# Pacing the row gathers of a mixture-of-experts kernel by TensorE's progress

## The chip, the cores and the metric

The kernel runs on one core of one Trainium2 chip. The metric is device time in microseconds (us) of one execution. Six participants matter: TensorE (PE in the profile, with its weight loads as PEld), VectorE (DVE), ScalarE (ACT), GpSimd (POOL), the SyncE queue (SP), and the 16 DMA engines that serve all the queues. Each engine works through its own instructions in order, and the engines wait for one another through semaphores.

## What is computed

An attention-like block (retention) is followed by a mixture of eight experts. The reference, cut to what matters:

```python
scores = scale * q @ k.T                       # 8 batches, 8 heads, 576 positions, 64 wide
x = ((scores * Dmat) @ v)                      # as 4608 tokens x 512
noisy = x @ w_gate + log1p(exp(x @ w_noise)) * noise
top2  = two best of 8 experts per token;  top2_w = softmax over the two
for e in range(8):
    h = maximum(x[mask] @ w1[e], 0)            # 512 -> 1024
    out[mask] += top2_w * (h @ w2[e])          # 1024 -> 512
```

Matmuls run in bf16. The noise and the weights decide which tokens an expert gets, so the rows of an expert are only known once the tokens have been routed.

## The kernel before

The attention part goes through 16 units (four pairs of batches, four pairs of heads). After each pair of batches the tokens of that pair are routed (`route`): the two best experts are found, each token gets a place in its experts' lists, the lists are turned into a table of row numbers `xi0` to `xi3`, and the token rows (512 bf16 values and 8 words of payload with the gate weights and places) are written to a scratch tensor `xd` in HBM. The fourth routing is the last; only then are all lists complete.

An expert has room for 1216 tokens, cut into nine pieces of 128 and one of 64. `tiles()` groups pieces into tiles. Nine early tiles of one or two pieces (experts 0 to 2, as far as their lists are sure to be filled by earlier routings) run while the attention part still goes on. Twenty late tiles of two to four pieces hold the other 65 pieces; they lie behind the last routing. `fetch` brings the rows of a tile's pieces together, one indirect DMA for each piece, issued by POOL (line 964 of the profile) into a place of class `xg`. There are 24 such places; the last routing uses ten of them first. TensorE transposes the rows (L982) and a copy makes the tile's `xT`; for experts 6 and 7 a DMA transpose on the SP queue (L972) does that instead. Then come the first product (`up`, L1036, for early tiles; `wide`, L1062, for late ones), the relu on ACT or DVE (L1045, L1047), and the second product (`second`, L1113), whose steps are woven between the first-product steps of the next tile. `finish` scales the result: rows of a token's first expert go to a second scratch tensor `yd` (L1147 or L1149, then L1153); rows of its second expert are added to what `prev` fetched back from `yd` (an indirect DMA of POOL, L1128, then L1157 on DVE) and are scattered to the output (an indirect DMA of POOL, L1161).

The order of the instructions is not written by hand. `Plan` records operations with a cost each, and `Plan.run` simulates the engines: it picks the operation that can begin first, gives it an engine and a place, and so fixes the order on every engine. What it fixes is the order alone. On the chip an instruction starts when its engine is free and its semaphores allow it, whether that is earlier or later than the simulated time.

Two details matter here. A gather in `fetch` waits for its table, for the written rows of `xd`, and for the last readers of its `xg` place. And `slot()` limits how many `xg` places the gathers may hold in the simulation: 14 while the routing still needs places, and afterwards a number that starts at 5 and grows by one for every two gathers placed:

```python
n = head[b.cls, b.stream]
lim = min(hi, 5 + (n - self.mark.setdefault((b.cls, b.stream), n)) // 2) if b.cls == "xg" else hi
```

Of the kernel before, what the change touches and what calls it, by code (L numbers as in the profile page):

```python
# [15 lines left out]
IOff = bass.IndirectOffsetOnAxis  # L16

P = 128
# [4 lines left out]
DM = 512  # L23
KD = DM // P
KF = F // P
# [4 lines left out]
YOFF = [sum(min(-(-x // P) * P, CAP) for x in FIRST[:e]) for e in range(E + 1)]  # L30
WAIT = (11, 14, 15)
CROSS = 6
CLOSE = ((256, 0, 0, 0, 0, 0, 0, 0), (512, 384, 384, 0, 0, 0, 0, 0), (768, 640, 512, 0, 0, 0, 0, 0))
PLW = 8
XW = DM // 2 + PLW
# [13 lines left out]


class Op:
    __slots__ = ("i", "eng", "fn", "prio", "dma", "port", "preds", "succ", "need", "allocs", "bufs", "fin", "on")


class Plan:
# [5 lines left out]
    BIAS = dict(DVE=1.5, ACT=0.5)  # L61

    def __init__(self):
        self.ops, self.slots, self.fifo, self.quota, self.zone, self.mark = [], {}, {}, {}, {}, {}

    def cls(self, name, tiles, **quota):
        self.slots[name] = [[0.0, None, t, p] for t, p in tiles]
# [6 lines left out]
    def fix(t=None):  # L74
        return Buf(None, None, t)

    def op(self, eng, cost, fn, r=(), w=(), prio=0.0, dma=0, after=(), port=False):
        o = Op()
        o.i, o.fn, o.prio, o.dma, o.port = len(self.ops), fn, prio, dma, port
        o.eng = eng if isinstance(eng, dict) else {eng: cost}  # L80
        o.succ, o.allocs, o.bufs = [], [], []
        preds = set(after)
        for items, wr in ((r, False), (w, True)):
            for it in items:
                b, sub = it if isinstance(it, tuple) else (it, None)
                for s2, o2, w2 in b.acc:
                    if (wr or w2) and (sub is None or s2 is None or s2 == sub):
                        preds.add(o2)
                if b not in o.bufs:
                    o.bufs.append(b)  # L90
        for items, wr in ((r, False), (w, True)):
            for it in items:
                b, sub = it if isinstance(it, tuple) else (it, None)
                if wr:
                    b.acc = [a for a in b.acc if a[1] is o or not (sub is None or a[0] == sub)]
                b.acc.append((sub, o, wr))
        preds.discard(o)
        for b in o.bufs:
            if b.cls is not None:
                if not b.ops:  # L100
                    o.allocs.append(b)
                    self.fifo.setdefault((b.cls, b.stream), []).append(b)
                b.ops.append(o)
                b.left += 1
        o.preds, o.need = preds, len(preds)
        for p in preds:
            p.succ.append(o)
        self.ops.append(o)
        return o

    def run(self):
        free, dma_free, port = {}, {}, [0.0]
        head = {k: 0 for k in self.fifo}
        used = {}
        lanes = {"SP": [], "POOL": []}
# [4 lines left out]
        def slot(b, taken):  # L120
            s = self.slots[b.cls]
            lim = self.quota[b.cls].get(b.stream, len(s))
            lo, hi = self.zone.get((b.cls, b.stream), (0, len(s)))
            if lim < len(s) and all(head[k] >= len(v) for k, v in self.fifo.items()
                                    if k[0] == b.cls and k[1] != b.stream):
                lo, hi = 0, len(s)
                n = head[b.cls, b.stream]
                lim = min(hi, 5 + (n - self.mark.setdefault((b.cls, b.stream), n)) // 2) if b.cls == "xg" else hi
            if used.get((b.cls, b.stream), 0) + sum(t[1].n for t in taken if t[1].cls == b.cls) + b.n > lim:
                return None  # L130
            ok = lambda x: x[1] is None and all(x is not y for t in taken for y in t[0])
            best = None
            for i, x in enumerate(s[:hi]):
                if i < lo:
                    continue
                if b.n == 2:
                    if i % 2 or not (ok(x) and ok(s[i + 1])):
                        continue
                    c, k = [x, s[i + 1]], (max(x[0], s[i + 1][0]), 0)
                elif not ok(x):  # L140
                    continue
                else:
                    c, k = [x], (x[0] + (0.3 if len(s) == 8 and ok(s[i ^ 1]) else 0.0), 1)
                if best is None or k < best[0]:
                    best = k, c
            return best and best[1]

        while ready:
            pick = None
            for o in ready:  # L150
                taken = []
                ok = all(b.cls is None or b.t is not None or b in o.allocs for b in o.bufs)
                if not ok:
                    continue
                for n, b in enumerate(o.allocs):
                    k = (b.cls, b.stream)
                    q = self.fifo[k]
                    m = len([t for t in taken if (t[1].cls, t[1].stream) == k])
                    if q[head[k] + m] is not b:
                        ok = False  # L160
                        break
                    x = slot(b, taken)
                    if x is None:
                        ok = False
                        break
                    taken.append((x, b))
                if not ok:
                    continue
                t0 = max([y[0] for x, b in taken for y in x], default=0.0)
                best = None  # L170
                for e, c in o.eng.items():
                    t = max(t0, free.get(e, 0.0))
                    if o.port and e in ("DVE", "POOL"):
                        t = max(t, port[0])
                    if o.dma and len(lanes[e]) >= 8:
                        t = max(t, lanes[e][-8])
                    for p in o.preds:
                        t = max(t, p.fin + (0.0 if p.on == e and not p.dma else self.LAT))
                    x = t + c + (self.BIAS.get(e, 0.0) if len(o.eng) > 1 else 0.0)
                    if best is None or x < best[0]:  # L180
                        best = x, e, t, c
                _, e, t, c = best
                key = (round(t * 20), o.prio, o.i)
                if pick is None or key < pick[0]:
                    pick = (key, o, e, t, c, taken)
            if pick is None:
                raise RuntimeError("no operation can go on: " + str([(o.i, o.prio) for o in ready[:20]]))
            _, o, e, t, c, taken = pick
            ready.remove(o)
            o.on = e  # L190
            free[e] = t + c
            if o.port and e in ("DVE", "POOL"):
                port[0] = t + c
            o.fin = t + c
            if o.dma:
                x = max(dma_free.get(e, 0.0), t + c)
# [37 lines left out]
class Kernel:  # L234
# [719 lines left out]
    def fetch(self, i, t, prio):  # L954

        pl, nc = self.pl, self.nc
        e, js, early = t
        ident = self.fixed["ident"]
        xi = self.fixed[f"xi{early}"]
        xg = [pl.buf("xg", "exp") for _ in js]  # L960
        rows = 1 + 1152 * (early + 1)
        for x, j in zip(xg, js):
            h, n = HPE * e + j, self.size(j)
            pl.op("POOL", 1.3, lambda _, x=x, h=h, n=n: nc.gpsimd.indirect_dma_start(  # L964
                out=x.t[:n, :], out_offset=None, in_=self.xd[:rows, :], in_offset=IOff(ap=xi.t[:n, h:h + 1], axis=0),
                bounds_check=rows - 1, oob_is_err=False), r=[xi] + self.xd_done[early], w=[x], prio=prio, dma=0.4)
        xT = pl.buf("half" if early < 3 else "big", "xt")
        w, m, off = sum(self.size(j) for j in js), len(js) * P, self.off(js)
        xv = lambda m=m: xT.t.bitcast(BF16)[:, :KD * m].rearrange("p (k s) -> p k s", k=KD)
# [5 lines left out]
        for c in range(0, 0 if e >= CROSS and early == 3 else len(js), 2):  # L975
            p = self.psum("xt")
# [72 lines left out]
    def wide(self, i, t, prio, g2=None):  # L1049
# [5 lines left out]
        for f in range(KF):  # L1055
            p = self.psum("exp")

            def pe(_, f=f, p=p):
                it = g2(f) if g2 else iter(())
                for di in range(KD):  # L1060
                    o = di * F + f * P
                    nc.tensor.matmul(p.t[:, :n], lhsT=w.t[:, o:o + P], rhs=xv()[:, di, :n],  # L1062
                                     start=(di == 0), stop=(di == KD - 1))
                    next(it, None)
                for _ in it:
                    pass
# [40 lines left out]
    def second(self, e, po, hT, c, f):  # L1107


        k = KF // len(hT)  # L1110
        hv = hT[f // k].t.bitcast(BF16).rearrange("p (f s) -> p f s", f=k)[:, f % k]
        o = KD * F + f * DM
        self.nc.tensor.matmul(po.t, lhsT=hv[:, c:c + P], rhs=self.W[e].t[:, o:o + DM],  # L1113
                              start=(f == 0), stop=(f == KF - 1))

    def prev(self, i, t, prio):
        pl, nc = self.pl, self.nc
# [53 lines left out]
    def record(self):  # L1171
# [32 lines left out]
        for i, t in enumerate(ts):  # L1204
            starts.setdefault(t[0], i)
        last = {t[0]: i for i, t in enumerate(ts)}
        ne = len([t for t in ts if t[2] < 3])
        landed = lambda u: [o for o in pl.ops if o.dma and o.prio == u]
        for e, u in enumerate(WAIT):
            self.weights(e, 40 + e, True, landed(u))  # L1210
# [200 lines left out]
```

## Time and profile before

| what | value |
| --- | --- |
| median of 3 runs | 490.4 us (485.36, 490.4, 490.55) |
| the profiled execution | 485.52 us, span from first to last instruction 484.0 us |
| PE busy | 398.0 us, 82% of the span |
| POOL busy | 292.9 us, 61% |
| ACT busy | 246.4 us, 51% |
| DVE busy | 187.5 us, 39% |
| mean granted TensorE clock | 0.926 of full speed |
| gathers of L964 | 80, of 1045 ns each on POOL |
| DMA | 105.32 MB, 218 GB/s over the span |

The page's busy shares are means over very different stages: attention up to about 180 us, the end of the early tiles up to about 228 us, the late tiles up to about 474 us, and a tail of scatters. "Busy" of POOL for an indirect DMA is the time in which POOL prepares the transfer, not the transfer itself. In the view of instructions in order of time, the bracket at the end of a row tells how long the engine had been idle before that row and what ended the wait: an engine and line, a DMA, "issue" (nothing that the profile shows), or "remote" (a semaphore whose update the profile can't put down to an instruction near it).

### The profile page before, as it was taken

The page shows a single profiled execution, that of the slowest core. Times are in us where ns is not written, and L with a number is a line of the kernel's source. Part 1 is how long each engine was busy: PE and PEld are TensorE (multiplying, and loading weights), DVE is VectorE, ACT ScalarE, POOL GpSimd, SP SyncE. Part 2 cuts the span into 40 slices and gives each one's busy share as a digit, 9 for nine tenths or more (in the row PEclk, how much of TensorE's full clock was granted, in tenths as well). Part 3 has the DMA queues.
Part 4 walks back from the last instruction along what each step waited for, and adds up shares of the span by engine and source line. Part 5 has one row for each costly group of instructions (what it writes and reads, how often), then busy time and mean ns, then how long its engine had stood idle before and what let it go on. Part 6 is the DMA issues. An engine that isn't in the chain of part 4 may idle for free. (4 is left out here: it accounts for less than half of the span.)

```text
span 484.0 us, 10610 instructions
## 1 busy us (share of the span) xinstructions
PE 398.0 (82%) x4032; PEld 245.5 (51%) x4032; DVE 187.5 (39%) x499; ACT 246.4 (51%) x431; POOL 292.9 (61%) x361
## 2 busy tenths in 40 slices
PE   1698768729988898149999888999799979999991
PEld 1576657528766665026565434455354434454450
DVE  2755776855892782001133313215025021031231
ACT  3699758657874743026575354745345233244320
POOL 8985779874497365733007747544656746656524
PEclk9889769878999999569999989999999979999997
DMA  7999999999599595423189977695599996645414
GB/s 192 298 261 286 272 238 303 257 245 328 128 319 269 136 256 166 96 75 118 37 291 349 343 248 220 188 369 166 167 310 298 236 217 182 181 150 161 150 55 144
DMA packets 102488, 105.32 MB, mean 218 GB/s; under 512 B 31870, under 2 KB 80511, under 8 KB 102434
## 3 DMA queue, kind: packets, MB, share of 16 engines
q1 hardware_dynamic: 80082, 58.92, 41.8%
q0 software_dynamic: 15264, 36.89, 30.2%
q10 hardware_dynamic: 7088, 8.80, 5.2%
q8 instruction: 32, 0.52, 0.5%
q14 instruction: 22, 0.18, 0.1%
HBM read 83.20 MB, written 26.63 MB: 227 GB/s over the span
## 5 line engine op out<-in xcount | busy, mean ns | idle before, releaser
L1113 PE MATMUL ps<-W,half 128*128 128x512 bf16 x640 | 214.9, 388 | 24.6 <-ACT half L1045 18.1
L1062 PE MATMUL ps<-big,W 128*128 128x512 bf16 (+4 forms) x640 | 190.5, 331 | 5.8 <-issue 5.2
L1045 ACT ACTIVATE half<-ps 128x512 bf16<-128x512 f32 (+5 forms) x180 | 87.1, 505 | 158.2 <-PE ps L1062 70.2
L964 POOL DMA_INDIRECT xg<-xd,xi x80 | 83.6, 1045 | 57.0 <-issue 20.4
L1113 PEld LDWEIGHTS <-half 128*128 128x128 bf16 x640 | 62.2, 99 | 99.4 <-ACT half L1045 18.9
L1062 PEld LDWEIGHTS <-W 128*128 128x128 bf16 x640 | 63.1, 99 | 55.5 <-issue 9.1
L1157 DVE SCALAR_TENSOR_TENSOR half<-ps,xg,half 128x512 f32<-128x512 f32 (+1 forms) x39 | 29.0, 747 | 73.5 <-PE ps L1113 42.1
L1161 POOL DMA_INDIRECT out_dram<-half,xg x39 | 39.1, 1003 | 29.6 <-issue 16.6
L1128 POOL DMA_INDIRECT half<-yd,xg x39 | 39.8, 1022 | 11.9 <-issue 11.9
L515 DVE TENSOR_TENSOR half<-ps,mask 128x512 bf16<-128x512 f32 x64 | 40.1, 682 | 16.4 <-PE ps L507 14.4
L269 ACT ACTIVATE half<-ps 128x1024 bf16<-128x1024 bf16 (+1 forms) x36 | 35.1, 990 | 15.5 <-PE ps L482 9.3
L457 POOL TENSOR_TENSOR half<-big,tab 128x1024 bf16<-128x1024 f32 x16 | 31.0, 1935 | 14.6 <-PE ps L482 6.2
L464 POOL TENSOR_TENSOR half<-big,tab 128x512 bf16<-128x512 f32 x32 | 33.6, 1066 | 1.5 <-issue 1.5
L542 PE MATMUL ps<-half,half 128*128 128x128 bf16 (+1 forms) x128 | 30.2, 322 | 2.4 <-POOL half L464 2.2
L1157 DVE SCALAR_TENSOR_TENSOR half<-ps,gm,half 128x512 f32<-128x512 f32 x6 | 4.5, 751 | 70.9 <-ACT half L1147 64.4
L1036 PE MATMUL ps<-half,W 128*128 128x256 bf16 (+1 forms) x288 | 29.1, 255 | 2.9 <-ACT half L269 2.5
L482 PE MATMUL ps<-ident__69,half 128*128 128x128 bf16 x256 | 22.3, 247 | 11.0 <-ACT half L449 5.9
L544 PE MATMUL ps<-vz,half 128*128 128x128 bf16 x128 | 25.4, 251 | 6.3 <-ACT vz L269 4.6
L1147 ACT ACTIVATE half<-ps,xg 128x512 f32<-128x512 f32 (+1 forms) x29 | 19.9, 685 | 16.4 <-PE ps L1113 11.0
L1036 PEld LDWEIGHTS <-W 128*128 128x128 bf16 x288 | 24.0, 98 | 7.0 <-issue 3.4
L554 ACT ACTIVATE tb<-ps 64x256 bf16<-64x256 f32 x56 | 21.1, 376 | 11.0 <-PE ps L544 9.8
L482 PEld LDWEIGHTS <-half 128*128 128x128 bf16 x256 | 18.9, 113 | 12.0 <-ACT half L449 5.9
(177 smaller groups left out, 462.8 us busy)
## 6 DMA issues: line engine op xcount, KB each, us to landing
big<-in_moe_w_dram SPq DMA_DIRECT2D x40, 512.0 KB
big<-in_k_dram SPq DMA_DIRECT2D x32, 256.0 KB
big<-in_q_dram SPq DMA_DIRECT2D x16, 512.0 KB
big<-in_v_dram SPq DMA_DIRECT2D x32, 256.0 KB
yd<-half SPq DMA_DIRECT2D x26, 256.0 KB
W<-in_moe_w_dram POOLq DMA_DIRECT2D x12, 512.0 KB
xd<-xg ACTq DMA_DIRECT2D x16, 264.0 KB
yd<-half ACTq DMA_DIRECT2D x15, 256.0 KB
```

What stands on the lines that cost most here:

```text
L269: self.nc.scalar.activation(out, in_, Act.Copy)
L464: self.eng(e).tensor_tensor(o, i, t, Alu.mult)
L482: nc.tensor.transpose(v[:, hp, x, :], i[:, y, hp * P:(hp + 1) * P], ident.t)
L515: nc.vector.tensor_tensor(S.t.bitcast(BF16).rearrange("p (h c x) -> p h c x", h=2, c=2)[:, h], p[h].t.rearrange("p (c x) -> p c x", c=2), ...
L964: pl.op("POOL", 1.3, lambda _, x=x, h=h, n=n: nc.gpsimd.indirect_dma_start(out=x.t[:n, :], out_offset=None, in_=self.xd[:rows, :], in_offs ...
L1036: nc.tensor.matmul(pv()[:, f2, :], lhsT=w.t[:, o:o + P], rhs=xv()[:, di, :n], start=(di == 0), stop=(di == KD - 1))
L1045: self.nc.scalar.activation(o, i, Act.Relu)
L1062: nc.tensor.matmul(p.t[:, :n], lhsT=w.t[:, o:o + P], rhs=xv()[:, di, :n], start=(di == 0), stop=(di == KD - 1))
L1113: self.nc.tensor.matmul(po.t, lhsT=hv[:, c:c + P], rhs=self.W[e].t[:, o:o + DM], start=(f == 0), stop=(f == KF - 1))
L1128: pl.op("POOL", 1.3, lambda _, b=b, iy=iy, n=self.size(j): nc.gpsimd.indirect_dma_start(out=b.t[:n, :], out_offset=None, in_=self.yd[:rows ...
L1157: pl.op("DVE", 0.75, lambda _, o=o, b=b, po=po, g=g, n=n: nc.vector.scalar_tensor_tensor(o.t[:n], po.t[:n], g()[:n], b.t[:n], Alu.mult, Al ...
L1161: ins = nc.gpsimd.indirect_dma_start(out=self.out[:, :], out_offset=IOff(ap=io()[:n], axis=0), in_=o.t[:n, :], in_offset=None, bounds_chec ...
```

## The change

The growing limit on `xg` places is removed: once the last routing has taken its places, gathers may hold all 24. In its place comes a pace for the gathers of late tiles other than the first late one (61 of the 80). In the simulation such a gather begins no sooner than 2.2 us after the last paced one. In the program it also waits for the matmul of L1062 or L1113 that was issued last ahead of it in the simulated order: `wide` and `second` note their newest matmul in `self.mm`, and `fetch` adds a semaphore dependency of the gather on it.

```diff
+PACE = 2.2
...
     def run(self):
-        free, dma_free, port = {}, {}, [0.0]
+        free, dma_free, port, paced = {}, {}, [0.0], 0.0
...
                 lo, hi = 0, len(s)
-                n = head[b.cls, b.stream]
-                lim = min(hi, 5 + (n - self.mark.setdefault((b.cls, b.stream), n)) // 2) if b.cls == "xg" else hi
+                lim = hi
...
                 t0 = max([y[0] for x, b in taken for y in x], default=0.0)
+                if o.pace:
+                    t0 = max(t0, paced + o.pace)
...
             free[e] = t + c
+            if o.pace:
+                paced = t
...
-            pl.op("POOL", 1.3, lambda _, x=x, h=h, n=n: nc.gpsimd.indirect_dma_start(
-                out=x.t[:n, :], out_offset=None, in_=self.xd[:rows, :], in_offset=IOff(ap=xi.t[:n, h:h + 1], axis=0),
-                bounds_check=rows - 1, oob_is_err=False), r=[xi] + self.xd_done[early], w=[x], prio=prio, dma=0.4)
+            pace = PACE if early == 3 and i > self.ne else 0.0
+
+            def get(_, x=x, h=h, n=n, pace=pace):
+                ins = nc.gpsimd.indirect_dma_start(
+                    out=x.t[:n, :], out_offset=None, in_=self.xd[:rows, :], in_offset=IOff(ap=xi.t[:n, h:h + 1], axis=0),
+                    bounds_check=rows - 1, oob_is_err=False)
+                if pace:
+                    self.tc.add_manual_dep(ins.ins, self.mm.ins.name, mybir.DependencyInfo(
+                        mybir.DependencyClass.Sync, mybir.DependencyReason.DATA), reason="gathers go at TensorE's pace")
+            pl.op("POOL", 1.3, get, r=[xi] + self.xd_done[early], w=[x], prio=prio, dma=0.4, pace=pace)
...
-                    nc.tensor.matmul(p.t[:, :n], lhsT=w.t[:, o:o + P], rhs=xv()[:, di, :n],
-                                     start=(di == 0), stop=(di == KD - 1))
+                    self.mm = nc.tensor.matmul(p.t[:, :n], lhsT=w.t[:, o:o + P], rhs=xv()[:, di, :n],
+                                               start=(di == 0), stop=(di == KD - 1))
...
-        self.nc.tensor.matmul(po.t, lhsT=hv[:, c:c + P], rhs=self.W[e].t[:, o:o + DM],
-                              start=(f == 0), stop=(f == KF - 1))
+        self.mm = self.nc.tensor.matmul(po.t, lhsT=hv[:, c:c + P], rhs=self.W[e].t[:, o:o + DM],
+                                        start=(f == 0), stop=(f == KF - 1))
```

`self.ne` is the number of early tiles (9), so the late tile with index 9 keeps its four gathers unpaced. The cost that the simulation puts on a gather (1.3 us of POOL) is unchanged.

More of the change, by code (lines that the diff above doesn't have):

```diff
@@ L51 @@
 class Op:
-    __slots__ = ("i", "eng", "fn", "prio", "dma", "port", "preds", "succ", "need", "allocs", "bufs", "fin", "on")
+    __slots__ = ("i", "eng", "fn", "prio", "dma", "port", "preds", "succ", "need", "allocs", "bufs", "fin", "on", "pace")
 class Plan:
@@ L63, in __init__ @@
     def __init__(self):
-        self.ops, self.slots, self.fifo, self.quota, self.zone, self.mark = [], {}, {}, {}, {}, {}
+        self.ops, self.slots, self.fifo, self.quota, self.zone = [], {}, {}, {}, {}
     def cls(self, name, tiles, **quota):
@@ L75, in fix, with op @@
         return Buf(None, None, t)
-    def op(self, eng, cost, fn, r=(), w=(), prio=0.0, dma=0, after=(), port=False):
+    def op(self, eng, cost, fn, r=(), w=(), prio=0.0, dma=0, after=(), port=False, pace=0.0):
         o = Op()
-        o.i, o.fn, o.prio, o.dma, o.port = len(self.ops), fn, prio, dma, port
+        o.i, o.fn, o.prio, o.dma, o.port, o.pace = len(self.ops), fn, prio, dma, port, pace
         o.eng = eng if isinstance(eng, dict) else {eng: cost}
@@ L1206, in record @@
         last = {t[0]: i for i, t in enumerate(ts)}
-        ne = len([t for t in ts if t[2] < 3])
+        self.ne = ne = len([t for t in ts if t[2] < 3])
         landed = lambda u: [o for o in pl.ops if o.dma and o.prio == u]
```

## Prediction

> **What bounds the kernel now.** I first read the page's chain of work that ended last. It covers nothing here, so it names no bound:
>
> ```profile
> span 484.0 us, 10610 instructions
> POOL 0%; issue 0%; POOLq 0%
> ```
>
> So I went to the busy times by stage. A row holds the window, its length, and then the busy time and count of PE, PEld, DVE, ACT and POOL, the granted clock, the DMA share and GB/s.
>
> ```profile
> 192.00:212.00 20.00, 2.19 (x5) 0.39 (x6) 0.52 (x4) 1.96 (x4) 12.89 (x13) 0.56 0.35 88
> 212.00:228.00 16.00, 16.00 (x126) 10.16 (x126) 1.03 (x6) 8.37 (x15) 3.98 (x4) 0.91 0.32 100
> 228.00:474.00 246.00, 233.81 (x1312) 119.13 (x1309) 64.02 (x111) 107.32 (x197) 132.52 (x128) 0.98 0.71 216
> 474.00:484.00 10.00, 0.00 (x0) 0.00 (x0) 0.75 (x1) 0.00 (x0) 3.89 (x5) 0.68 0.35 124
> ```
>
> From 212 to 474 PE is the bound: it is busy 249.8 of 262 us, and every other engine has half its time free or nearly so. The last 10 us are a tail of scatters in which PE does nothing. The row that stands out is the first. For 20 us PE does 2.19 us of work, ACT and DVE do next to nothing, and only POOL works. In the order of time these are the PE, ACT and POOL rows around it (start, busy time, and in brackets the idle time before and what ended it):
>
> ```profile
> 191.40 0.49 PE L1036 MATMUL ps<-half,W 128*128 128x256 bf16 x3 [0.35 <-issue]
> 194.97 1.04 PE L1113 MATMUL ps<-W,half 128*128 128x512 bf16 x2 [3.08 <-issue]
> 203.43 1.04 PE L1113 MATMUL ps<-W,half 128*128 128x512 bf16 x2 [7.42 <-ACT half L1045]
> 211.88 4.18 PE L1113 MATMUL ps<-W,half 128*128 128x512 bf16 x12 [7.42 <-ACT half L1045]
> 194.31 0.60 ACT L1045 ACTIVATE half<-ps 128x512 bf16<-128x512 f32 x1 [3.72 <-remote]
> 202.78 0.60 ACT L1045 ACTIVATE half<-ps 128x512 bf16<-128x512 f32 x1 [7.86 <-remote]
> 211.23 1.08 ACT L1045 ACTIVATE half<-ps 128x512 bf16<-128x512 f32 x2 [7.86 <-remote]
> 184.26 0.96 POOL L964 DMA_INDIRECT xg<-xd,xi  x1 [5.45 <-DVE half L1047]
> 207.59 1.00 POOL L964 DMA_INDIRECT xg<-xd,xi  x1 [0.31 <-issue]
> L964 POOL DMA_INDIRECT xg<-xd,xi x19 | 18.8, 992 | 10.9 <-DVE half L1047 5.5 <-issue 5.2 <-DMA xg<-xd,xi 0.3
> ```
>
> PE waits for a relu of ACT (L1045). ACT waits for the signal that the first-product matmuls are done, and those had been issued by 191.9 (191.40 + 0.49). The last two relus stand in one row at 211.23: their signals came together, although their matmuls are different ones. So the matmuls were not late; the word of them was. In the same time POOL issues 19 gathers with nothing between them, from 184.26 to 208.59, one every 1.30 us ((207.59 - 184.26) / 18). The relus are freed one by one, 8.46 us apart (six or seven gathers), and the last one 2.6 us after the chain's end.
>
> Does that happen elsewhere? I looked for ACT waits ended by "remote" in the late tiles, and for what POOL did before them; and, as a control, for an isolated gather.
>
> ```profile
> ACT half L1045 <- remote: 38.2, 7, 8.5
> 266.06 1.00 POOL L964 DMA_INDIRECT xg<-xd,xi  x1 [0.30 <-issue]
> 279.07 1.00 POOL L964 DMA_INDIRECT xg<-xd,xi  x1 [0.30 <-remote]
> 278.88 0.44 ACT L1045 ACTIVATE half<-ps 128x320 bf16<-128x320 f32 x1 [8.53 <-remote]
> 279.37 0.30 PE L1062 MATMUL ps<-big,W 128*128 128x320 bf16 x1 [2.10 <-issue]
> 333.92 1.05 POOL L1161 DMA_INDIRECT out_dram<-half,xg  x1 [1.83 <-DVE W L271]
> 345.91 1.00 POOL L964 DMA_INDIRECT xg<-xd,xi  x1 [0.30 <-issue]
> 348.31 0.60 ACT L1045 ACTIVATE half<-ps 128x512 bf16<-128x512 f32 x1 [2.25 <-remote]
> 348.96 0.38 PE L1113 MATMUL ps<-W,half 128*128 128x512 bf16 x1 [2.47 <-ACT half L1045]
> 371.65 1.05 POOL L964 DMA_INDIRECT xg<-xd,xi  x1 [0.30 <-issue]
> 388.70 1.00 POOL L964 DMA_INDIRECT xg<-xd,xi  x1 [0.30 <-issue]
> 391.96 1.09 ACT L1045 ACTIVATE half<-ps 128x512 bf16<-128x512 f32 x2 [5.68 <-remote]
> 217.06 1.00 POOL L964 DMA_INDIRECT xg<-xd,xi  x1 [1.30 <-ACT half L1147]
> 218.72 0.60 ACT L1045 ACTIVATE half<-ps 128x512 bf16<-128x512 f32 x1 [0.28 <-PE ps L1036]
> ```
>
> Three more unbroken chains of POOL's indirect DMAs (266.06 to 280.07, 333.92 to 346.91, 371.65 to 389.70; 10 to 14 transfers each) have such a late relu in them or up to 2.3 us behind. The lone gather at 217.06 has none: the relu behind it waits 0.28 us for PE, by name. The seven waits of the summary make 38.2 us of ACT; PE, which has other work at most of them, loses far less. That is a correlation at four places with a control, not a proof. It is what my forecast rests on: **a long unbroken chain of POOL's indirect DMAs holds back PE's signals to ACT.**
>
> **The change part by part.**
>
> *The chain behind the last routing breaks up.* In the changed program 61 of the 80 gathers wait for a matmul. The paced gathers number 20 to 40 wait for matmuls that lie, on the mean, 2.1 us of PE work apart, and all 61 are let go within some 184 us of PE work, 3.0 us apart. Both are longer than the 1.30 us of the chain. Since the matmul waited for stands in PE's order, a stalled PE now stops the gathers, so a chain can't run on while PE stands. Only the first four gathers after the routing are unpaced, and some three more wait for matmuls that are done by then: about seven run from 184.3 to 192 before POOL halts. So I let the first idle gap of PE (3.08) stay, and take away the two of 7.42: **-14.8 us**. The bounds are 0 (nothing goes) and -17.9 (3.08 goes too).
>
> *The clock.* After the hole PE runs slower than it does a little later:
>
> ```profile
> 219.40 3.62 PE L1113 MATMUL ps<-W,half 128*128 128x512 bf16 x16
> ```
>
> Twelve matmuls took 4.18 us at 211.88 (0.348 each) and sixteen took 3.62 here (0.226 each); the windows show the clock granted at 0.56 in the hole and 0.91 behind it. Twelve times 0.122 is **-1.5 us**, if the clock no longer falls. Bounds 0 to -1.5.
>
> *The late tiles.* From 228 to 474 PE is idle for 12.2 us (246 - 233.81). The two gaps shown at 279.37 and 348.96 make 4.6 of it. The new order still has runs of up to six of `prev` and scatter (L1128, L1161), which are not paced, so I take a third of the 12.2: **-4.0 us**. Bounds 0 to -12.2.
>
> *The gathers wait, and POOL with them.* The waits stand in POOL's queue, so the `prev` and scatter behind a halted gather halt too, and behind these the add on DVE (L1157), the free `xg` places, and the writes of `yd` on SP and ACT as far as they share buffers. In the late window POOL is busy 132.52 of 246, so 113 us are free, 1.85 us for each of the 61 paced gathers. Each gather is let go at least 10 us of matmul work ahead of the transposes that read its rows, and a tile's last gather some 196 matmuls ahead of the tile's first product. The trace has no such wait; the nearest row is a gather that waited for its `xg` place:
>
> ```profile
> 214.76 0.99 POOL L964 DMA_INDIRECT xg<-xd,xi  x1 [6.17 <-ACT half L1147]
> ```
>
> POOL stood for 6.17 us there and PE was fully busy in that window (16.00 of 16.00), so a stand of that size has been absorbed once. I put this part at **0**; its upper bound is the second rival's price.
>
> *Moved steps.* Four gathers of an early tile move ahead of the last routing's steps on POOL:
>
> ```profile
> 173.71 1.11 POOL L964 DMA_INDIRECT xg<-xd,xi  x1 [0.17 <-issue]
> 177.75 1.05 POOL L964 DMA_INDIRECT xg<-xd,xi  x1 [0.30 <-issue]
> 163.07 0.24 POOL L737 TENSOR_TENSOR d<-bm,am 128x9 f32<-128x9 f32 x1 [4.12 <-DVE bm L714]
> ```
>
> Three fit into the 4.12 us that POOL idles at 163.07; one falls between two routing steps and may cost up to 1.3 us, which POOL gets back where they stood before (173.71 to 178.80). Three writes of `yd` move ahead of transposes on SP's queue. No row shows PE waiting for either, so both go at **0**, the gather with a bound of +1.3. PE's signals grow from 634 to 646 and POOL's separate waits from 217 to 227, on queues with idle time: 0.
>
> **Sum**, against the profiled execution's own 485.5 us (span 484.0 and 1.5 around it): 485.5 - 14.8 - 1.5 - 4.0 + 0 = 465.2, so **465 us**. That execution lies 4.9 us below the median of the three runs and equals the fastest of them; I keep to it, since its rows carry the sum.
>
> **The rivals.**
>
> *The gathers are innocent* (or the new waits find their matmuls already done and change nothing). The relus were late for a reason of their own, the gathers merely filled the time, and the hole stays: the time is **485 us**. For it: no row shows how a gather could hold a signal back. Against it: the four chains, and the control. The Trainium skill, SBUF — State Buffer, section "SBUF: two separate sides", speaks for this rival: "Engine ports and AXI ports are disjoint. A DMA cannot be slowed by a compute op, and vice versa." By that rule gathers cost ACT nothing, and the sum would be 485. The trace differs with it as far as the 8.53 us wait at 278.88 falls inside a chain.
>
> *POOL now waits for the late word itself* (slower). If PE's signals are late for whatever reason, the gathers, which need PE's signal now, hear of it late as well, and POOL, which is in order, loses that time 61 times. It decides from 1.85 us per gather, the free time above; beyond that `prev`, scatters and gathers fall behind PE. Releases came 1.4 us (346.91 to 348.31) to 2.6 us (208.59 to 211.23) after a chain's end. At 2.5 us the excess is 61 x 0.65 = 40 us, on top of the 465: **about 504 us**. For it: ACT lost 38.2 us to this kind of wait, seven times, and it waits for PE as POOL now will. Against it: without chains no late word was seen (218.72), and the waits of neighbouring gathers overlap.
>
> *Half of it stays* (a smaller gain). The first seven gathers and the copies of the routing before them already make a chain long enough for one more period of 8.46 us: 465 + 8.5, **about 473 us**.
>
> **How the numbers follow.** Forecast 0.68, gathers innocent 0.12, POOL late 0.12, half of it stays 0.08. A change of 1% (4.9 us) is about what a measurement of this kernel can tell from none. Faster by over 1%: 0.68 + 0.08 = 0.76. Within 1%: the innocent case, 0.12, less 0.01 for a small loss by the moved gather, so 0.11. Slower: 0.12 + 0.01 = 0.13. The forecast's own range: below, the whole 17.9, 1.5 and about 11 of the late 12.2 go (455); above, 3.08 and the late idle stay and the moved gather costs 1.3 (about 470). For 8 in 10 it has to take in half-stays and the innocent case with the spread of the runs: **455 to 487**; only the slow rival lies outside.
>
> **What would show it.** Right: between 184 and 215 no chain of over eight gathers; the L1045 rows there released by PE by name, with idle times under 1 us; the window 192 to 212 with PE busy over 15 us and a clock near 0.9; L964 waiting for PE (L1062, L1113) 61 times with POOL's busy time unchanged; the window of the late tiles shorter by about 4 us. Wrong: relus still 8.46 us apart in an intact hole though POOL halts (innocent); or L1128, L1161 and the transposes of L982 (L993 in the changed kernel) waiting on gathers, with PE idle over 20 us in the late tiles (POOL late). A single gap of about 8 us behind 184 shows the half case.

## The result, and the profile after

The changed kernel takes 466.22 us (median of four runs, 464.33 to 468.77), the kernel before 488.17 us in the same comparison (four runs): a ratio of 0.959, 95% interval 0.953 to 0.964. Some executions of a kernel are slower than the others of the same kernel; the medians in this document take in all runs and the ratios leave the slow ones out, so the two need not agree exactly. The profiled execution of the changed kernel is the longest of its four runs (468.77 us, span 467.2).

These are the stages of the changed kernel, with the columns of the table of before (window, its length, then busy time and count of PE, PEld, DVE, ACT and POOL, clock, DMA share, GB/s):

```profile
192.00:212.00 20.00, 17.08 (x125) 10.36 (x124) 0.52 (x4) 8.37 (x17) 8.73 (x9) 0.91 0.42 123
212.00:228.00 16.00, 16.00 (x103) 8.77 (x101) 1.63 (x6) 10.48 (x19) 6.70 (x7) 1.00 0.31 83
228.00:456.00 228.00, 214.56 (x1229) 110.56 (x1227) 63.23 (x110) 99.89 (x181) 134.29 (x131) 0.99 0.73 231
456.00:467.00 11.00, 1.15 (x6) 0.30 (x4) 1.23 (x2) 0.00 (x0) 5.09 (x6) 0.75 0.42 152
```

In the 20 us behind 192, PE does 17.08 us of work where it did 2.19, at a clock of 0.91 where 0.56 was granted. The late tiles end 18 us earlier. From 228 us on, PE still idles 13.4 us inside them (228 - 214.56); it was 12.2 before.

The same place in order of time: PE, then ACT's relus (now L1056), then POOL's gathers (now L971).

```profile
194.39 0.61 PE L1124 MATMUL ps<-W,half 128*128 128x512 bf16 x2 [0.68 <-issue]
197.24 4.08 PE L1124 MATMUL ps<-W,half 128*128 128x512 bf16 x12 [2.24 <-ACT half L1056]
193.74 0.60 ACT L1056 ACTIVATE half<-ps 128x512 bf16<-128x512 f32 x1 [1.52 <-PE ps L1047]
196.59 1.09 ACT L1056 ACTIVATE half<-ps 128x512 bf16<-128x512 f32 x2 [2.25 <-remote]
203.53 0.60 ACT L1056 ACTIVATE half<-ps 128x512 bf16<-128x512 f32 x1 [0.28 <-PE ps L1047]
186.57 1.04 POOL L971 DMA_INDIRECT xg<-xd,xi  x1 [9.73 <-DVE half L1058]
194.48 0.99 POOL L971 DMA_INDIRECT xg<-xd,xi  x1 [0.30 <-issue]
198.12 0.95 POOL L971 DMA_INDIRECT xg<-xd,xi  x1 [2.65 <-PE ps L1124]
202.08 0.99 POOL L971 DMA_INDIRECT xg<-xd,xi  x1 [3.01 <-issue]
```

Seven gathers run from 186.57 to 195.47, and the eighth then stands for a matmul of L1124 until 198.12. Two gaps of PE are left, 0.68 and 2.24 us, where there were 17.92 us (3.08 + 7.42 + 7.42). Once the gathers come singly or in pairs, the relus follow PE by name with a wait of 0.28 us.

### The profile page after: what moved, and what is told of

It reads as the page before. It is cut to its first block, busy times and chain, and to the rows that moved or that the text cites. A ratio compares the mean times of both kernels' runs of the same rounds, so it can differ in the third digit from the quotient of the medians.

```text
span 467.2 us, 10624 instructions
## 1 busy us (share of the span) xinstructions
PE 393.9 (84%) x4032; PEld 244.6 (52%) x4032; DVE 187.3 (40%) x501; ACT 247.5 (53%) x429; POOL 292.0 (62%) x361
## 5 line engine op out<-in xcount | busy, mean ns | idle before, releaser
L1124 PE MATMUL ps<-W,half 128*128 128x512 bf16 x640 | 211.5, 383 | 10.5 <-issue 5.6
L1056 ACT ACTIVATE half<-ps 128x512 bf16<-128x512 f32 (+5 forms) x176 | 84.9, 504 | 135.5 <-PE ps L1073 63.4
L971 POOL DMA_INDIRECT xg<-xd,xi x80 | 82.9, 1036 | 68.2 <-issue 21.7
L1124 PEld LDWEIGHTS <-half 128*128 128x128 bf16 x640 | 61.9, 98 | 87.9 <-issue 14.0
L1172 POOL DMA_INDIRECT out_dram<-half,xg x39 | 38.8, 996 | 35.5 <-issue 19.9
L1139 POOL DMA_INDIRECT half<-yd,xg x39 | 42.1, 1079 | 11.9 <-issue 11.6
L1047 PE MATMUL ps<-half,W 128*128 128x256 bf16 (+1 forms) x288 | 31.2, 264 | 3.0 <-ACT half L273 2.6
L486 PE MATMUL ps<-ident__69,half 128*128 128x128 bf16 x256 | 21.3, 240 | 12.3 <-ACT half L453 6.4
L546 PE MATMUL ps<-half,half 128*128 128x128 bf16 (+1 forms) x128 | 29.2, 314 | 2.7 <-POOL half L468 2.5
L1158 ACT ACTIVATE half<-ps,xg 128x512 f32<-128x512 f32 (+1 forms) x27 | 18.5, 687 | 16.8 <-PE ps L1124 9.2
L486 PEld LDWEIGHTS <-half 128*128 128x128 bf16 x256 | 17.8, 109 | 13.6 <-ACT half L453 6.4
```

What stands on the lines that cost most here:

```text
L486: nc.tensor.transpose(v[:, hp, x, :], i[:, y, hp * P:(hp + 1) * P], ident.t)
L971: ins = nc.gpsimd.indirect_dma_start(out=x.t[:n, :], out_offset=None, in_=self.xd[:rows, :], in_offset=IOff(ap=xi.t[:n, h:h + 1], axis=0), ...
L1047: nc.tensor.matmul(pv()[:, f2, :], lhsT=w.t[:, o:o + P], rhs=xv()[:, di, :n], start=(di == 0), stop=(di == KD - 1))
L1056: self.nc.scalar.activation(o, i, Act.Relu)
L1124: self.mm = self.nc.tensor.matmul(po.t, lhsT=hv[:, c:c + P], rhs=self.W[e].t[:, o:o + DM], start=(f == 0), stop=(f == KF - 1))
L1139: pl.op("POOL", 1.3, lambda _, b=b, iy=iy, n=self.size(j): nc.gpsimd.indirect_dma_start(out=b.t[:n, :], out_offset=None, in_=self.yd[:rows ...
```

## The experiments

The theory (called the chain theory): an unbroken chain of POOL's indirect DMAs holds back PE's signals. Its rivals: the gain comes from the new order and the gathers are innocent; or a busy POOL holds the signals, whatever it does. The runs fell on three chips, each group at its own time. Four kernels shared one chip, on which the kernel before took 489.63 us; four shared a second (487.36); the last four shared a third, on which the kernel before took 446.71, and that matters below. Line numbers shift a little with each edit; the names of the tiles tell which operation a row shows.

**The new order without the waits.**

```diff
-                if pace:
+                if False:
                     self.tc.add_manual_dep(ins.ins, self.mm.ins.name, ...
```

> The changed kernel with the same order on every engine, but without the 61 semaphore waits. Chain theory (an unbroken chain of POOL's indirect DMAs holds PE's signals back): the gathers run in a chain behind the routing again, 19 or more at 1.30 us, the hole of about 18 us comes back, about 484 us. Order theory (the gain came from the new order, for instance from the four gathers that moved ahead of the last routing; the gathers are innocent): no hole, about 467 us.

Measured: 498.13 us, ratio to before 1.014 (1.009 to 1.020). ACT's relus, the ends of POOL's chain and PE's gaps in its trace:

```profile
196.68 0.60 ACT L1056 ACTIVATE half<-ps 128x512 bf16<-128x512 f32 x1 [2.92 <-remote]
201.68 0.60 ACT L1056 ACTIVATE half<-ps 128x512 bf16<-128x512 f32 x1 [4.40 <-remote]
212.23 0.60 ACT L1056 ACTIVATE half<-ps 128x512 bf16<-128x512 f32 x1 [9.95 <-remote]
186.57 1.04 POOL L971 DMA_INDIRECT xg<-xd,xi  x1 [9.57 <-DVE half L1058]
210.00 1.00 POOL L971 DMA_INDIRECT xg<-xd,xi  x1 [0.30 <-issue]
197.34 0.61 PE L1124 MATMUL ps<-W,half 128*128 128x512 bf16 x2 [3.46 <-issue]
202.33 1.04 PE L1124 MATMUL ps<-W,half 128*128 128x512 bf16 x2 [4.39 <-issue]
212.89 1.46 PE L1124 MATMUL ps<-W,half 128*128 128x512 bf16 x3 [9.52 <-issue]
```

With the order of the changed kernel and no waits the 19 gathers run in a chain again (186.57 to 211.00), and the hole is back: 3.46 + 4.39 + 9.52 = 17.4 us. The order theory falls. The time is 14 us above what the chain theory expected. PE's gaps of half a microsecond and more in the late tiles add up to 19.9 us here and to 10.5 in the kernel before. This order has its own long chains there (12 transfers from 262.8, 14 from 373.1), but the order before had such chains too, so that they are the reason is likely and not shown.

**The old order with the waits.** The growing limit and no planned pace, and the 61 waits.

```diff
-                lim = hi
+                n = head[b.cls, b.stream]
+                lim = min(hi, 5 + (n - self.mark.setdefault(...)) // 2) if b.cls == "xg" else hi
...
-            pl.op("POOL", 1.3, get, ..., dma=0.4, pace=pace)
+            pl.op("POOL", 1.3, get, ..., dma=0.4)
```

> The kernel before with its growing limit and its order, and the waits alone added (each late gather but the first four waits for the matmul of L1062 or L1113 issued last ahead of it). Chain theory: the chain stops after about seven gathers, the two idle gaps of 7.42 go, about 468 us. Order theory: the hole stays, about 485 us.

Measured: 478.62 us, ratio 0.975 (0.969 to 0.980). The window behind the routing, and the largest gap that is left (the PE row, and the DVE row that it waits behind):

```profile
190.00:212.00 22.00, 20.03 (x164) 13.68 (x168) 1.80 (x6) 12.43 (x22) 6.93 (x7) 1.00 0.36 112
242.68 0.34 PE L1074 MATMUL ps<-big,W 128*128 128x192 bf16 x1 [9.66 <-DVE big L276]
239.34 0.16 DVE L1012 TENSOR_TENSOR gm<-xg 128x1 f32<-128x1 f32 x1 [22.12 <-DMA xg<-xd,xi]
```

The hole is gone, so the waits alone break it. The gathers of that window come in groups of three and four, 1.30 us apart inside a group, and no relu there waits over 1.52 us: a short group at the narrow pitch held nothing back. But 9.66 us are lost further on. DVE stands for the rows of a gather (22.12 us), and the copy of the transposes that PE needs stands behind that in DVE's queue. In the old order the gathers lie close ahead of the work that reads them; held to PE's progress, some come late. So the change has two halves that need each other: the waits break the chain, and the new order places the gathers early enough to bear the waits. By the ratios the first half alone is worth about 12 us here (0.025 of 489.63), and the second alone costs about 7 (0.014). The new order itself comes from two edits, the lifted limit and the planned pace of 2.2; no run has one without the other.

**Twice the instructions, the same bytes.** In the kernel before. The second DMA fetches the piece's first 64 rows again, so this kernel leaves out the other 64:

```diff
+                for a in (0, 64) if 0 < k <= 19 and n == P else (0,):
+                    m = 64 if 0 < k <= 19 else n
                     nc.gpsimd.indirect_dma_start(
-                out=x.t[:n, :], ... ap=xi.t[:n, h:h + 1]
+                        out=x.t[a:a + m, :], ... ap=xi.t[:m, h:h + 1]
```

> The kernel before, in which each of the first 19 late pieces is gathered by two indirect DMAs of 64 rows in place of one of 128 (the second repeats the first 64 rows, so that the same bytes move; the repeated rows are wrong rows). Chain theory with the number of instructions as the dose: the chain lasts about 19 x 1.3 = 25 us longer, the hole grows by about that, about 510 us. If the bytes or descriptors are the dose: the hole stays near 18 us, about 486 us. If the gathers are innocent: about 486 us, with a hole of 18 us that ends long before the chain does.

Measured: 508.91 us, ratio 1.036 (1.027 to 1.046). First and last transfer of the chain, and PE's gaps:

```profile
183.53 0.96 POOL L969 DMA_INDIRECT xg<-xd,xi  x1 [4.32 <-DVE half L1053]
225.91 0.95 POOL L969 DMA_INDIRECT xg<-xd,xi  x1 [0.30 <-issue]
194.99 0.61 PE L1119 MATMUL ps<-W,half 128*128 128x512 bf16 x1 [3.99 <-issue]
209.77 1.04 PE L1119 MATMUL ps<-W,half 128*128 128x512 bf16 x2 [14.18 <-issue]
231.47 1.03 PE L1119 MATMUL ps<-W,half 128*128 128x512 bf16 x2 [20.66 <-ACT half L1051]
```

The chain has 35 transfers and lasts 43.3 us in place of 24.3 with 19; the hole is 38.8 us in place of 17.9. Sixteen more instructions cost 20.9 us, 1.31 each, close to the pitch of the chain (1.30 us before, 1.25 here). The dose is the number of instructions, or the time that they take, and not the bytes. Innocent gathers would have left the hole where it was.

**Room between the gathers, and no wait.** In the kernel before, behind each of the first 19 late gathers:

```diff
+                if 0 < k <= 19:
+                    s = self.fixed["olo"].t
+                    nc.gpsimd.tensor_tensor(s[:, 8:12], s[:, 0:4], s[:, 4:8], Alu.mult)
```

> The kernel before, with a VectorE-style multiply of 128 x 512 elements on POOL (about 1.1 us, no DMA, result unused) behind each of the first 19 late gathers; no wait for PE. Chain theory with the pitch as the dose: gathers come every 2.4 us or so, the signals arrive in between, the hole shrinks to under 6 us, about 470 us. If a busy POOL as such holds the signals: the hole grows with the chain to about 19 x 2.4 = 46 us, about 510 us. If the gathers are innocent: the hole stays at 18 us, about 486 us.

Measured: 480.04 us, ratio 0.978 (0.969 to 0.986).

```profile
190.00:212.00 22.00, 21.66 (x171) 14.48 (x172) 2.59 (x5) 13.48 (x24) 20.38 (x19) 1.00 0.41 127
187.55 1.04 POOL L967 DMA_INDIRECT xg<-xd,xi  x1 [0.16 <-issue]
188.61 1.17 POOL L972 TENSOR_TENSOR olo<-olo 128x512 f16<-128x512 f16 x1
189.94 1.03 POOL L967 DMA_INDIRECT xg<-xd,xi  x1 [0.16 <-issue]
216.71 1.65 PE L1069 MATMUL ps<-big,W 128*128 128x448 bf16 x4 [4.90 <-DVE big L271]
242.39 0.34 PE L1069 MATMUL ps<-big,W 128*128 128x192 bf16 x1 [7.32 <-DVE big L271]
```

POOL is busy for 20.38 of 22 us and PE for 21.66: the hole is gone although POOL rests less than before. A gather every 2.39 us (187.55 to 189.94) with a multiply behind it holds nothing back; 19 in a row, one every 1.30 us, did. So neither a busy POOL nor the waits as such are what counts, but the unbroken chain. Whether the wider pitch breaks it, or an instruction of another kind between two transfers, isn't separated: the multiply does both. The time missed the expected 470 by 10 us, for the reason seen above: in the old order the delayed gathers now come late, and PE idles 4.90 and 7.32 us behind DVE.

**What is left, on the second chip.** First the changed kernel again, as a measure:

> The changed kernel again, as the measure for the three others on the same chip: about 466 us by any theory.

Measured: 467.31 us, ratio 0.947 (0.935 to 0.959). Then the first late tile's gathers paced as well (`i >= self.ne`):

> The changed kernel with the four gathers of the first late tile paced as well. Chain theory: the seven gathers that still ran in a row behind the routing break up, and the gaps of PE of 0.68 and 2.24 us at 193.7 to 197.2 go: about 3 us below the changed kernel, some 463 us. Rival (these gaps belong to the first late tile's own order, not to the chain; or its rows now come late): 466 us or above.

Measured: 463.21 us, ratio 0.947 (0.937 to 0.956): not told apart from the changed kernel. Its trace does show what was expected behind the routing, where the changed kernel on this chip had a gap of 3.06 us:

```profile
192.00:212.00 20.00, 19.99 (x166) 12.80 (x164) 2.13 (x10) 12.05 (x22) 8.87 (x9) 1.00 0.47 143
```

Then `prev` and the scatters with the same wait (`add_manual_dep` on `self.mm` in both):

> The changed kernel, in which the 39 fetches from yd and the 39 scatters wait as well for the matmul of L1062 or L1113 issued last ahead of them; planner's times unchanged. Chain theory: the mixed chains of POOL that remain between 338 and 394 us break up, and part of the 9.0 us of PE gaps there (2.81, 0.90, 3.73, 1.55) goes: about 4 us below the changed kernel, some 462 us. Rival (those gaps come from rows that arrive late, not from held signals): no gain or a loss, 466 to 475 us.

Measured: 459.64 us, ratio 0.940 (0.931 to 0.949). The medians lie as expected, but the intervals of the ratios overlap, so a gain over the changed kernel isn't shown. Of the four gaps that PE had between 364 and 397 us in the first profile of the changed kernel (9.0 us together), its trace has one left, of 2.79 us. Last, a planned pitch of 1.7 for all three kinds:

> All three kinds of late indirect DMA wait for the matmul issued last ahead of them, and the planner keeps 1.7 us between any two of them (first late tile's gathers included). Chain theory: no unbroken chain is left, both the 2.9 us at 194 and most of the 9.0 us between 364 and 397 go: some 456 us. Rival (late rows; POOL too slow for the work with a pitch of 1.7): 466 to 480 us, with PE waiting for the transposes.

Measured: 468.72 us, ratio 0.963 (0.953 to 0.973), no better than the changed kernel. Its summary of waits has the reason in one row (us in total, times, longest):

```profile
PE ps L1074 <- DMA big<-xg: 13.3, 1, 13.3
```

PE waits 13.3 us for the DMA transposes of one tile of the last experts, whose gathers were pushed back behind `prev` and scatters. The late-rows rival decides here.

**The third chip.** The kernel before took 446.71 us here (11 runs), over 40 us less than on the other two.

> The kernel with all three kinds of late indirect DMA waiting for PE (as in the run before), and the first late tile's gathers paced too; planner's pace 2.2 for gathers alone. Chain theory: the 3.04 us gap of PE at 191 goes as well: about 3 us below the 459.6 of the run without the first tile, some 457 us. Rival (the two edits repair the same loss, or the first late tile gets its rows late): 460 us or above.

> The same with a planner's pace of 1.7 for the gathers, which places them earlier against the tiles that read them, but lets runs of gathers come nearer to the 1.30 of a chain. If what is left is rows that come late: 453 to 456 us. If the pitch still has to be wide: longer chains, 460 to 466 us.

Measured: 452.08 us, ratio 1.012 (1.008 to 1.016), and 451.32 us, ratio 1.013 (1.008 to 1.017): both slower than before. What was expected had been worked out from the second chip and can't be held against these times. The order without waits, with 26 multiplies in their place:

> The changed kernel's order without its 61 waits, and in their place a multiply of 128 x 512 elements on POOL (1.16 us) behind each of the first 26 late gathers. If the pitch of the indirect DMAs is what counts: the hole of 17.4 us behind the routing goes, the gaps of the later tiles stay, 498 - 17.4 - 1.5 = about 479 us. If only waiting for PE helps: about 498 us or more.

Measured: 458.54 us, ratio 1.026 (1.022 to 1.030). The expected figure was made for another chip here too. But its trace has a longer chain than any other: 41 indirect DMAs, from the first row below to the second, and nothing between them but pauses of some 0.30 us and one of 0.51. The third row is a relu inside the chain, the fourth a window over all of it.

```profile
338.02 1.02 POOL L1174 DMA_INDIRECT out_dram<-half,im  x1 [3.24 <-DVE half L1170]
392.74 1.02 POOL L1141 DMA_INDIRECT half<-yd,xg  x1 [0.31 <-issue]
380.16 0.60 ACT L1058 ACTIVATE half<-ps 128x512 bf16<-128x512 f32 x1 [1.18 <-PE ps L1075]
338.00:394.00 56.00, 54.99 (x293) 27.11 (x291) 14.04 (x20) 24.12 (x45) 43.34 (x41) 1.00 0.94 258
```

PE is busy for 54.99 of 56 us, and the relus follow PE by name. A busy PE alone would prove little: the changed kernel, in its first profile, has a chain of 17 from 337.44 to 362.38 (one transfer of it takes 3.91 us) in which PE doesn't idle either. But there the relus lose their beat at the chain's end. They start at 355.30 and 357.03, 1.73 us apart, and then 2.47 and 2.87 later:

```profile
337.40:362.40 25.00, 25.00 (x124) 11.61 (x123) 7.07 (x11) 10.94 (x20) 20.05 (x17) 1.00 0.83 275
359.50 0.60 ACT L1056 ACTIVATE half<-ps 128x512 bf16<-128x512 f32 x1 [1.29 <-PE ps L1124]
362.37 0.60 ACT L1056 ACTIVATE half<-ps 128x512 bf16<-128x512 f32 x1 [2.27 <-PE ps L1124]
```

On the third chip the same steps keep the beat inside the chain (357.35, 359.08, 360.81, 362.53, 364.26). The place behind the routing says the same. With a planned pitch of 1.7, seven gathers run in a row on the second chip (183.56 to 192.45) and PE loses 2.64 us in two gaps; eight run in a row on the third (181.54 to 191.69), and PE has no gap there. The first row is a relu on the second chip, the second one on the third:

```profile
192.18 0.60 ACT L1057 ACTIVATE half<-ps 128x512 bf16<-128x512 f32 x1 [2.90 <-remote]
188.77 0.60 ACT L1057 ACTIVATE half<-ps 128x512 bf16<-128x512 f32 x1 [0.28 <-PE ps L1048]
```

In the four kernels traced on the third chip no relu of ACT waits for "remote"; in each of the ten traces from elsewhere between one and twelve do. So what the chain theory describes holds on the two chips above and in the first two profiles, and no trace of the third chip shows it. Whether the chip is the reason, or something else that differed between the groups of runs, isn't shown.

It roughly fits the time of before here: 485.5 less the 30.1 us that PE idles in the hole and the late tiles of the first profile (17.9 + 12.2), less the 8.9 us by which PE's busy time is lower on this chip (389.1 in the profiled execution of the first of these runs, 398.0 in that of before), is 446.5. That is an estimate. It puts all of the late idle down to chains, which no run shows, and takes PE's busy time from another kernel, so that it comes so near to 446.71 is partly chance. Before wasn't traced here, and the changed kernel wasn't run here.

Last, a pace that is too wide (`PACE = 3.0` in the changed kernel):

> The changed kernel with a planner's pace of 3.0 in place of 2.2: 61 gathers need 183 us, nearly all of the 228 us of late tiles. Chain theory alone: chains get no longer, 464 to 468 us. Late-rows rival: the margin of at least 10 us of matmul work between a gather and the transposes shrinks away, PE waits for transposes (L993) and for DMA transposes, 470 to 485 us.

Measured: 482.01 us, ratio 1.080 (1.076 to 1.084).

```profile
PE ps L993 <- DMA xg<-xd,xi: 16.0, 5, 4.4
PE ps L1073 <- DMA big<-xg: 8.4, 1, 8.4
327.30 0.61 PE L993 MATMUL ps<-ident__69,xg 128*128 128x128 bf16 x4 [4.39 <-DMA xg<-xd,xi]
```

PE waits 16.0 us for gathered rows in five places, and 8.4 us for a DMA transpose, and the time is 30 us above that of the two paced kernels with 2.2 and 1.7 on the same chip (these also let `prev`, the scatters and the first late tile wait). The late-rows rival is right here; in the changed kernel, with 2.2, PE's summary of waits has no wait for such a DMA.

## Why the prediction was right, and where not

**The bound and its cause: right, on the chips that have it.** The prediction rested on a correlation at four places. The added instructions (20.9 us for 16), the spacers (no hole with POOL busier) and the order without waits (hole back) show that the unbroken chain causes the hole. "That the gathers are innocent", given 0.12, is out for those chips.

**The gap term, -14.8: right, also in its mechanism.** Seven gathers and then a halt were expected, with 3.08 us of gap left; seven came, and 2.92 us are left (0.68 + 2.24), so the term measured -15.0.

**The clock, -1.5: the cause was not where it was put.** The twelve matmuls behind the gaps, which were to gain the 1.5 us, still take 4.08 us (4.18 before), with a gap of only 2.24 us ahead of them. PE's busy time did fall, from 398.0 to 393.9 us, and the clock of the window rose from 0.56 to 0.91:

```profile
PE 393.9 (84%) x4032; PEld 244.6 (52%) x4032; DVE 187.3 (40%) x501; ACT 247.5 (53%) x429; POOL 292.0 (62%) x361
```

So 4.1 us came from matmuls that ran faster, over the whole program; the runs don't say how much of it is the hole's.

**The late tiles, -4.0: wrong.** PE's idle time there went up by 1.2 us (12.2 to 13.4). The old gaps at 279 and 349 are gone, but gathers, `prev` and scatters still make long chains together, and PE has other gaps. Around the end of one of 12 transfers:

```profile
378.67 1.01 POOL L1172 DMA_INDIRECT out_dram<-half,xg  x1 [2.95 <-DVE half L1168]
393.09 1.00 POOL L1139 DMA_INDIRECT half<-yd,xg  x1 [0.30 <-issue]
396.52 1.57 ACT L1056 ACTIVATE half<-ps 128x512 bf16<-128x512 f32 x3 [1.56 <-remote]
395.01 0.39 PE L1124 MATMUL ps<-W,half 128*128 128x512 bf16 x1 [3.73 <-issue]
397.17 0.61 PE L1124 MATMUL ps<-W,half 128*128 128x512 bf16 x1 [1.55 <-ACT half L1056]
```

The prediction took the chains of `prev` and scatter as six long, from the order of the instructions. That counted the transfers between two gathers; but a paced gather whose matmul is long done breaks no chain. On the chip 12 stood unbroken here, and 17 at 337.44. Besides, the third of 12.2 us was a guess at what chains cost there. Two of the chains that it shows begin earlier than its rows (13 transfers from 261.83, 16 from 366.77), and it left out two of 12 transfers (405.44 to 420.93 and 437.49 to 452.91) in which PE, with other work to do, didn't idle. The first of them, in the kernel before:

```profile
405.00:421.00 16.00, 16.00 (x76) 7.24 (x75) 2.40 (x4) 5.71 (x11) 12.13 (x12) 1.00 0.64 174
```

**The waits at 0, and "POOL waits for the late word itself": right to leave it small.** POOL's busy time is unchanged (292.0 us over the program, 292.9 before). The waits of gathers for PE, by the summary:

```profile
POOL xg L971 <- PE ps L1073: 8.5, 7, 2.7
POOL xg L971 <- PE ps L1124: 7.6, 6, 2.6
```

Thirteen named waits, 16.1 us in all, none over 2.7 us; the expected 61 named waits don't appear; the other gathers found their matmul done, or their wait was put down to another releaser. Where the waits did cost time, it was not the signal that was late but the rows: with the old order (a gap of 9.66 us), with the pitch of 1.7 for all three kinds (13.3), and on the third chip with a pace of 3.0 (16.0). In the changed kernel no such wait of PE is seen.

**The sum.** In the profiled execution: -15.0 for the hole, -4.1 for faster matmuls, +1.2 in the late tiles, and +0.9 of PE's idle time before 192 us and in the tail together, is -17.0; measured by the two times, 485.52 - 468.77 = 16.75. The forecast had 20.3 off; two terms of it were off in opposite directions (the clock by 2.6 too little, the late tiles by 5.2 too much). The median of the runs, 466.22, came nearer to 465 than the profiled execution did, and that is partly luck: the two errors were opposite, and the forecast started from an execution 2.7 us below the median of before in this comparison (488.17).

**The rule that spoke for innocent gathers.** The prediction weighed the Trainium skill's rule (SBUF — State Buffer, "SBUF: two separate sides") that a DMA can't be slowed by a compute operation and vice versa. On the third chip the rows agree: inside 41 transfers PE idles 1.0 us of 56. On the others a chain of transfers does hold engines up, and the rule would have given 485 us. Nothing here says that SBUF's ports are the place where this happens.

## What to carry to other kernels

Where an engine waits for a signal whose matmuls were issued long before, look at what the queue of indirect DMAs did just then: 19 of them with a multiply between each two (a pitch of some 2.4 us) held nothing back, and 19 in an unbroken chain of 24.3 us, one every 1.3 us, cost PE 17.9 us. What a chain costs depends on what else PE has to do: inside chains of 12 and 17 among the late tiles it didn't idle. A wait on another engine's progress spaces transfers well, but only if they are planned early enough to bear it: the waits with late places lost 9.66 us again, and too wide a pace left PE waiting 16.0 us for rows. And compare on more than one chip: on the third, where no trace shows a held signal, the paced kernels were 1.2 to 8.0% slower than the one before the change.

## What was not expected of the hardware

PE's signals are late, ACT's to PE are not. In the hole of the kernel before, the relu at 202.78 ends at 203.38 and PE starts at 203.43, so ACT's signal to PE takes 0.05 us at the very time at which ACT waits 7.86 us for PE's. Why PE's signals wait and why the third chip's traces don't show it stays open: no run looked inside. It is also open what the changed kernel itself takes on the third chip.
